# Chunk-selecting attention with a gated feed-forward layer on one core: the last block product of the program, made, added and stored in two halves of 128 columns

## The chip, the core and the metric

The program runs on one core of a Trainium2 chip. A core has five engines with a queue of instructions each: TensorE (PE in the profile; its weight loads are shown as PEld), VectorE (DVE), ScalarE (ACT), GpSimd (POOL) and SyncE (SP), which here issues nearly all transfers. Engines wait for each other through semaphores. The metric is the time of one execution on the device in microseconds (us); less is better.

## The reference, cut to what matters

```python
B, H, S, D = 4, 8, 768, 64                     # batch, heads, sequence, head dimension
# attention: each query keeps the 6 chunks of 32 keys with the highest upper bound
k_min, k_max = k_chunks.min(axis=3), k_chunks.max(axis=3)
ub = np.sum(np.maximum(q * k_min, q * k_max), axis=-1)      # causal chunks only
mask = sel & (pos[:, None] >= pos[None, :])                 # sel: the top 6 by ub
attn = softmax(where(mask, q @ k.T / 8, -1e9))
x = (attn @ v)                                 # -> 3072 tokens x 512
# feed-forward: 512 -> 1536 -> 512
gate = 1 / (1 + np.exp(-(x @ w_gate)))
out = (gate * (x @ w_val)) @ w_out             # 3072 x 512, float32
```

## The kernel before

The 3072 tokens are cut into eight units, u0 to u7, of three blocks of 128 tokens. A unit goes through chunk choice, attention and feed-forward (`ffn`, line 1239). The units' work is interleaved: a text, `ORDER`, lists every operation of the program with its engine, and the operations are issued in exactly that order. A second text, `SLOTS`, gives every tile its buffer; for most operations of TensorE this is one of the eight accumulator banks. A third text, `TIES`, adds some waits by hand. No scheduler decides anything at build time except which waits follow from these texts.

The last product of the feed-forward layer, hidden values times `w_out`, is done for units 4 to 7 on pairs of token blocks (`pair`, line 1058). Two blocks of 128 tokens times 512 columns are treated as a 2 by 2 scheme of blocks, which needs seven products instead of eight: p1, p2, p6, p5, p3, p7, p4, each with sums of hidden values (made at line 1069 into the tiles `sw` and `sx`) or of weights (`tw`). A product (line 1082) is six matmuls of 128 by 128 weights with 256 columns, which add up in one bank. VectorE then adds it onto the output tile `ox` or `sw` (function `onto`, line 1099; "c22", "c21" and so on are the names of these additions). The last pair of the program is called u67: the third blocks of units 6 and 7. The end of `ORDER` before is

```
p7_u67=P p7z_u67=P c22_u67=V out_u67_b1=S p4_u67=P p4z_u67=P c21_u67=V out_u67_1=S
```

so the last things that the program does are: product p7, the addition c22 (512 columns, as two lots of 256), the store `out_u67_b1` of the right half of the last 128 rows, product p4 (issued in two parts, `p4` and `p4z`, of four and two matmuls), the addition c21 of 256 columns, and the store `out_u67_1` of the left half of these rows. c21 reads and writes a quarter of `ox` that c22 has written, so it follows c22.

A store (line 1127) is one transfer issued on SP. Each transfer that SP issues is counted by one of eight completion counters, DMAHW0 to DMAHW7, taken in turn. Where a counter's earlier transfer has to be waited for as well, SP has a small wait instruction ahead of the transfer.

After the last store comes a closing stage that the framework adds (line 1452 in the profile, the end of the program). SP waits there for everything, two semaphores to an instruction and one instruction after another, in this order:

```
1 DMASW7, DMASW6    2 DMAHW0, DMASW5    3 DMAHW1, DMASW4
4 DMAHW2, DMASW3    5 DMAHW3, DMASW2    6 DMAHW4, DMASW1
7 DMAHW5, DMASW0    8 DMAHW6, DVE       9 DMAHW7, ACT
```

(DMASW are the counters of the transfers that GpSimd issues.) Then the five engines meet twice and the execution ends. In the program before, `out_u67_b1` is counted by DMAHW6 and the very last store, `out_u67_1`, by DMAHW7.

Of the kernel before, what the change touches and what calls it, by code (L numbers as in the profile page):

```python
# [262 lines left out]
c22_u67=V out_u67_b1=S p4_u67=P p4z_u67=P c21_u67=V out_u67_1=S  # L263
# [51 lines left out]
sc_u4_7_0:0 att_u4_7:2 sc_u4_7_1:4 pv_u4_3:1 sc_u4_7_2:4 sc_u4_7_3:2 rz_u4_3:0 x_u4_3:1 g_u4_0:3 gate_u4_0:0 v_u4_0:5 hg_u4_0:6
g_u4_1:7 gate_u4_1:2 v_u4_1:2 g_u4_2:3 gate_u4_2:1 v_u4_2:1 hg_u4_1:5 g_u4_3:3 gate_u4_3:3 v_u4_3:1 g_u4_4:6 gate_u4_4:0 v_u4_4:4
hg_u4_2:7 g_u4_5:6 gate_u4_5:2 v_u4_5:3 g_u4_6:6 gate_u4_6:2 v_u4_6:1 hg_u4_3:1 g_u4_7:7 gate_u4_7:3 v_u4_7:4 g_u4_8:7 gate_u4_8:0
v_u4_8:5 hg_u4_4:2 g_u4_9:3 gate_u4_9:1 v_u4_9:4 g_u4_10:7 gate_u4_10:1 v_u4_10:6 hg_u4_5:8 g_u4_11:6 gate_u4_11:2 v_u4_11:1
held:0 sw:1 p1_u4:7 p26_u4:1 p5_u4:7 p3_u4:2 p7_u4:4 p4_u4:6 k_3:0 q_3:1 kx_3:1 k16_3_0:4 kt_3_0:6 k16_3_1:2 kt_3_1:1 k16_3_2:3
# [77 lines left out]
def pe(busy, lag=170):  # L397
    return {PE: (busy, busy + lag)}
# [1058 lines left out]
```

## Time and profile before

| | |
|---|---|
| median of 3 runs | 281.0 us (280.67 to 282.69) |
| profiled execution: its time / its span | 279.88 us / 278.2 us |
| TensorE busy | 269.2 us, 97% of the span |
| VectorE, ScalarE, GpSimd busy | 231.2, 180.4, 163.1 us |
| granted TensorE clock | 1.0 |

The span runs from the first to the last instruction that the profiler saw; 1.7 us of the profiled execution's time lie outside it. Busy shares are averages over very different stages. For a change at the very end of the program the last few microseconds of the trace matter, and there the order of single instructions.

### The profile page before, as it was taken

Reading aid. Unit: us, or ns where it says so; the run is one execution under the profiler, and the core shown is the slowest. Engines: PE = TensorE matmul, PEld = TensorE weight load, DVE = VectorE, ACT = ScalarE, POOL = GpSimd, SP = SyncE. Lnnn points to the kernel's source line nnn. Section 1 sums busy time; section 2 is a strip of 40 time slices with the busy share of each in tenths; the row PEclk is TensorE's granted clock in tenths of the full one; section 3 lists DMA queues with packets and bytes.
Section 4 is the critical chain, followed back from the end, with each engine's and each line's share of the span. In section 5 each row is a group of like instructions: output and inputs, shape, how many; then the busy total and the mean of one; then the engine's idle time right before and its main releaser. Section 6 shows DMA issues by size and latency. Waiting matters only on the chain.

```text
span 278.2 us, 7566 instructions
## 1 busy us (share of the span) xinstructions
PE 269.2 (97%) x2806; PEld 189.3 (68%) x2806; DVE 231.2 (83%) x686; ACT 180.4 (65%) x386; POOL 163.1 (59%) x262
## 2 busy tenths in 40 slices
PE   5979999999999999999999999999999999999995
PEld 3755658667755666557687657776888688778684
DVE  4799747687999998796999987978889998888985
ACT  6388969569858944468689979988983422341430
POOL 5797744639372873534669966724766467163440
PEclk9999999999999999999999999999999999999999
DMA  6999999999999598696896230100320033000304
GB/s 157 258 281 204 207 217 208 220 179 202 187 217 189 142 183 188 145 161 125 164 157 114 68 85 17 40 0 3 73 77 2 1 83 127 2 1 2 151 2 152
DMA packets 131717, 34.70 MB, mean 125 GB/s; under 512 B 119776, under 2 KB 128736, under 8 KB 131680
## 3 DMA queue, kind: packets, MB, share of 16 engines
q1 hardware_dynamic: 126912, 29.50, 50.6%
q0 software_dynamic: 4768, 4.72, 10.1%
q8 instruction: 22, 0.36, 0.5%
q14 instruction: 15, 0.12, 0.1%
HBM read 30.67 MB, written 6.29 MB: 133 GB/s over the span
## 4 chain that ended last, share of the span: by engine, by line
PE 87%; DMA 6%; DVE 5%; SPq 1%; issue 0%; POOL 0%; DVEq 0%
PE v_u L1259 20%; PE g_u L1259 15%; PE sc_u L957 12%; PE o_u L1308 11%; PE p_u L1082 10%; PE pv_u L990 7%; DMA wg<-in_moe_w_gate_dram 5%; PE p_g_u L1191 5%; PE ube_u L896 3%; DMA kf<-in_k_dram 1%; DVE xf L768 1%; PE kfT L709 1%; PE qfT L709 1%; PE fl L591 1%; DVE kx_u L681 1%; DVE kcr L681 1%
## 5 line engine op out<-in xcount | busy, mean ns | idle before, releaser
L968 ACT ACTIVATE att_u<-sc_u 128x512 f16<-128x512 f32 (+3 forms) x184 | 86.9, 573 | 8.6 <-PE sc_u L957 7.3
L1259 PE MATMUL v_u<-xT_u,wv 128*128 128x384 f16 x384 | 72.4, 326 | 0.0
L1280 DVE SCALAR_TENSOR_TENSOR hg_u<-gate_u,v_u 128x384 f16<-128x384 f16 x96 | 51.2, 545 | 19.3 <-ACT gate_u L1271 9.7
L1271 ACT ACTIVATE gate_u<-g_u 128x384 f16<-128x384 f32 x72 | 35.1, 499 | 40.3 <-PE g_u L1259 35.1
L1259 PE MATMUL g_u<-xT_u,wg 128*128 128x384 f16 x288 | 56.0, 326 | 0.9 <-ACT xT_u L452 0.5
L1259 PEld LDWEIGHTS <-wv 128*128 128x128 f16 x384 | 36.2, 98 | 20.3 <-issue 0.2
L974 POOL TENSOR_SCALAR_AFFINE_SELECT att_u<-att_u 128x384 f16<-128x384 f16 (+1 forms) x56 | 28.0, 509 | 37.4 <-ACT att_u L968 16.4
L1259 PEld LDWEIGHTS <-wg 128*128 128x128 f16 x288 | 26.7, 98 | 18.3 <-DMA wg<-in_moe_w_gate_dram 1.8
L1308 PE MATMUL o_u<-wo,hg_u 128*128 128x512 f16 x144 | 34.3, 379 | 0.0
L990 PE MATMUL pv_u<-v,att_u 128*128 128x65 f16 x640 | 26.3, 193 | 0.0
L990 PEld LDWEIGHTS <-att_u 128*128 128x128 f16 x640 | 24.2, 98 | 2.9 <-issue 0.6
L1228 DVE TENSOR_TENSOR f_g_u<-p_g_u,f_g_u 128x192 f32<-128x192 f32 (+1 forms) x72 | 24.9, 383 | 1.0 <-PE p_g_u L1191 0.4
L957 PE MATMUL sc_u<-hqe,hke 128*128 128x128 f16 (+2 forms) x220 | 25.1, 243 | 0.0
L957 PE MATMUL sc_u<-hqo,hko 128*128 128x128 f16 (+2 forms) x220 | 24.1, 243 | 0.0
L1308 PEld LDWEIGHTS <-hg_u 128*128 128x128 f16 x144 | 13.7, 98 | 13.4
L957 PEld LDWEIGHTS <-hke 128*128 128x128 f16 x220 | 16.5, 98 | 4.9 <-issue 0.6
L957 PEld LDWEIGHTS <-hko 128*128 128x128 f16 x220 | 16.4, 98 | 4.4
L673 POOL CAST v<-v 128x512 f16<-128x512 f32 x23 | 14.4, 627 | 5.8 <-DVE qf_u L863 1.8
L1271 ACT ACTIVATE gate_u<-f_g_u 128x384 f16<-128x384 f32 x24 | 11.9, 519 | 5.6 <-DVE hg_u L1280 2.9
L1011 DVE TENSOR_TENSOR x_u<-pv_u,rz_u 128x384 f16<-128x384 f32 (+1 forms) x28 | 14.6, 524 | 0.9 <-DMA xT_u<-x_u 0.6
L919 DVE MAX8 mx_u<-ubn_u 128x8 f32<-128x8 f32 (+16 forms) x152 | 12.7, 158 | 0.3
L1099 DVE SCALAR_TENSOR_TENSOR sw<-p_u,sw 128x256 f32<-128x256 f32 (+1 forms) x20 | 10.6, 528 | 2.4 <-PE p_u L1082 2.0
(187 smaller groups left out, 504.9 us busy)
## 6 DMA issues: line engine op xcount, KB each, us to landing
v<-in_v_dram SPq DMA_DIRECT2D x23, 256.0 KB, 4.7
k<-in_k_dram SPq DMA_DIRECT2D x12, 384.0 KB, 5.4
q<-in_q_dram SPq DMA_DIRECT2D x12, 384.0 KB, 5.9
out_dram<-osb_u SPq DMA_DIRECT2D x12, 256.0 KB, 3.3
out_dram<-sw SPq DMA_DIRECT2D x8, 256.0 KB, 2.1
wv<-in_moe_w_val_dram POOLq DMA_DIRECT2D x3, 512.0 KB, 9.8
wo<-in_moe_w_out_dram POOLq DMA_DIRECT2D x3, 512.0 KB, 17.6
qf<-in_q_dram SPq DMA_DIRECT2D x8, 128.0 KB, 3.3
```

The source lines that it names most:

```text
L673: plan.add(f"v16_{b}_{ib}", {POOL: pool(H * D)}, lambda e: nc.gpsimd.tensor_copy(v16[b % 2][:, ib, :, 0:D], at(t)), reads=[t], writes=[("v ...
L957: nc.tensor.matmul(at(t)[:, o:o + 128 * m], hk[b % 2][e_][:, p, 128 * jb:128 * jb + 128], hq[u.side][e_][:, p, 128 * x:128 * (x + m)], sta ...
L968: plan.add(f"exp_{u.name}_{h}_{y}", {ACT: act(n)}, lambda e, t=t, att=att, b0=b0, n=n: nc.scalar.activation(at(att)[:, b0:b0 + n], at(t), ...
L974: nc.gpsimd.affine_select(out=dv, in_=dv, compare_op=ALU.is_ge, fill=0.0, base=0, pattern=[[0, u.m], [1, 128]], channel_multiplier=-1)
L990: nc.tensor.matmul(at(pv)[:, last, x, :], at(att)[:, c:c + 128], v16[b % 2][:, jb, h, :], start=(jb == 0), stop=(jb == ib))
L1011: plan.add(f"x_{u.name}_{p}", {DVE: dve(u.t)}, lambda e: nc.vector.tensor_tensor(at(x_).rearrange("p a (e d) -> p e a d", e=2), at(pv)[:, ...
L1082: nc.tensor.matmul(at(to)[:, side], a(j)[:, i], b(j)[:, i], start=j == i == 0, stop=j == 2 and i == 1)
L1228: plan.add(f"{p}_{name}", {POOL: pool2(192 * n), DVE: dve(192 * n)} if slow else {DVE: dve(192 * n)}, lambda e: both(e).tensor_tensor(dst( ...
L1259: nc.tensor.matmul(at(t), w16[:, c, 128 * fb:128 * fb + 128], at(u.xt)[:, c, :], start=(c == 0), stop=(c == 3))
L1271: plan.add(f"tanh_{u.name}_{fb}", {ACT: act(T, not seven[0])}, lambda e, gv=gv, gate=gate: nc.scalar.activation(at(gate), gv(), AF.Tanh, s ...
L1280: plan.add(f"hg_{u.name}_{fb}", {DVE: dve(T)}, lambda e, vv=vv, gate=gate, hg=hg, fb=fb: nc.vector.scalar_tensor_tensor(at(hg)[:, fb % 2], ...
L1308: nc.tensor.matmul(at(o), at(hgs[fc // 2])[:, fc % 2, 128 * tb:128 * tb + 128], wo16[:, fc, lo:hi], start=(fc == 0), stop=(fc == NFB - 1))
```

## The change

The product p4 of pair u67 is made as two products of 128 columns, `p4` and `p4b`, each of six matmuls, in two accumulator banks. Each has its own addition (c21, c21b) of 128 columns and its own store (`out_u67_1`, `out_u67_1b`) of 128 rows by 128 columns, 64 KB. `out_u67_b1` stays as it was. Stores, products and additions of all other pairs stay as they were.

```diff
-c22_u67=V out_u67_b1=S p4_u67=P p4z_u67=P c21_u67=V out_u67_1=S
+c22_u67=V out_u67_b1=S p4_u67=P p4b_u67=P c21_u67=V c21b_u67=V out_u67_1=S out_u67_1b=S
...
         if name == "u67":
             store(f"{name}_b1", lambda: four()[:, 3], rows[1], 256, 512, [key[3]], next_)
-            store(f"{name}_1", lambda: four()[:, 2], rows[1], 0, 256, [key[2]], next_)
+            for side, cut, last in (("", slice(0, 128), p4), ("b", slice(128, 256), bank("p4b"))):
+                def emit(e, cut=cut, last=last):
+                    for j in range(3):
+                        for i in range(2):
+                            nc.tensor.matmul(at(last)[:, 0, cut], block(j, 1, 1)[:, i], t_(3)(j)[:, i, cut],
+                                             start=j == i == 0, stop=j == 2 and i == 1)
+                plan.add(f"p4{side}_{name}", pe(...), emit, reads=[...], writes=[last], prio=next_())
+                done = key[2] if side == "" else (okey, 2, side)
+                plan.add(f"c21{side}_{name}", {DVE: dve(128)}, lambda e, cut=cut, last=last: nc.vector.scalar_tensor_tensor(
+                    four()[:, 2, cut], at(last)[:, 0, cut], 0.5, four()[:, 2, cut], ALU.mult, ALU.add),
+                    reads=[last, key[2]], writes=[done], prio=next_(EV))
+                store(f"{name}_1{side}", lambda cut=cut: four()[:, 2, cut], rows[1], cut.start, cut.stop, [done], next_)
```

Up to the last product, no engine's order of operations changes. What does change in the whole program is `SLOTS`: 496 of its 1053 old entries have another number, nearly all of them accumulator banks. A bank decides which earlier tile has to be read out before a product may write. Setting the two built programs side by side, 65 of the 655 matmuls that wait for something wait for another event than before; on ScalarE one wait falls away, and on VectorE, GpSimd and SP nothing differs ahead of c21. Since the counters are taken in turn, the store `out_u67_1` is counted by DMAHW7 and the new last store, `out_u67_1b`, by DMAHW0.

More of the change, by code (lines that the diff above doesn't have):

```diff
@@ L316 @@
[L316 to L319, printed above, removed]
@@ new lines @@
+kT_u1_1:3 kt_u1_1:0 kn_u1_2:0 kT_u1_2:1 kt_u1_2:0 kn_u1_3:1 kT_u1_3:1 kt_u1_3:2 qn_u1_0:5 qT_u1_0:0 qf_u1:0 qm_u1:0 qn_u1_1:0
+qT_u1_1:5 qn_u1_2:4 qT_u1_2:6 qn_u1_3:6 qT_u1_3:0 ube_u1:5 ubo_u1:7 ubn_u1:0 mx_u1:0 apt_u1:0 g_u0_0:2 gate_u0_0:0 v_u0_0:3
+hg_u0_0:0 g_u0_1:6 gate_u0_1:3 v_u0_1:1 g_u0_2:4 gate_u0_2:1 v_u0_2:5 hg_u0_1:1 g_u0_3:0 gate_u0_3:2 v_u0_3:4 g_u0_4:6 gate_u0_4:0
+v_u0_4:0 hg_u0_2:3 g_u0_5:7 gate_u0_5:3 v_u0_5:2 g_u0_6:1 gate_u0_6:2 v_u0_6:3 hg_u0_3:2 g_u0_7:5 gate_u0_7:1 v_u0_7:4 g_u0_8:4
@@ new lines @@
+gate_u0_8:0 v_u0_8:7 hg_u0_4:5 g_u0_9:5 gate_u0_9:2 v_u0_9:6 g_u0_10:3 gate_u0_10:1 v_u0_10:0 hg_u0_5:4 g_u0_11:6 gate_u0_11:3
+v_u0_11:3 o_u0_0:4 osb_u0_0:0 o_u0_1:5 osb_u0_1:1 o_u0_2:0 osb_u0_2:0 kq_u2:1 v_0_4:5 v_0_5:4 kf_3:3 qf_3:1 vf_3:0 kn_u2_0:4
+kT_u2_0:5 kx_u2:0 kt_u2_0:0 kn_u2_1:0 kT_u2_1:7 kt_u2_1:1 kn_u2_2:6 kT_u2_2:6 kt_u2_2:1 kn_u2_3:0 kT_u2_3:1 kt_u2_3:2 qn_u2_0:3
+qT_u2_0:3 qf_u2:1 qm_u2:0 qn_u2_1:1 qT_u2_1:6 qn_u2_2:6 qT_u2_2:4 qn_u2_3:5 qT_u2_3:1 ube_u2:3 ubo_u2:7 ubn_u2:0 mx_u2:0 apt_u2:0
@@ new lines @@
+sc_u1_0_0:1 att_u1_0:1 sc_u1_0_1:2 sc_u1_0_2:6 sc_u1_1_0:7 att_u1_1:3 sc_u1_1_1:6 pv_u1_0:0 sc_u1_1_2:0 sc_u1_2_0:5 att_u1_2:2
+sc_u1_2_1:5 rz_u1_0:1 x_u1_0:0 xps_u1_0:1 xT_u1:1 sc_u1_2_2:0 sc_u1_3_0:1 att_u1_3:0 sc_u1_3_1:2 pv_u1_1:7 sc_u1_3_2:3 sc_u1_4_0:3
+att_u1_4:2 sc_u1_4_1:4 rz_u1_1:0 x_u1_1:2 xps_u1_1:4 sc_u1_4_2:5 sc_u1_5_0:4 att_u1_5:0 sc_u1_5_1:1 pv_u1_2:0 sc_u1_5_2:2
+sc_u1_6_0:4 att_u1_6:3 sc_u1_6_1:2 rz_u1_2:0 x_u1_2:1 xps_u1_2:2 sc_u1_6_2:7 sc_u1_7_0:3 att_u1_7:1 sc_u1_7_1:2 pv_u1_3:0
@@ new lines @@
+sc_u1_7_2:5 rz_u1_3:1 x_u1_3:2 xps_u1_3:0 g_u1_0:5 gate_u1_0:0 v_u1_0:7 hg_u1_0:6 g_u1_1:2 gate_u1_1:1 v_u1_1:5 g_u1_2:0
+gate_u1_2:2 v_u1_2:4 hg_u1_1:7 g_u1_3:0 gate_u1_3:3 v_u1_3:0 g_u1_4:1 gate_u1_4:0 v_u1_4:2 hg_u1_2:8 g_u1_5:0 gate_u1_5:0 v_u1_5:1
+g_u1_6:5 gate_u1_6:2 v_u1_6:3 hg_u1_3:0 g_u1_7:0 gate_u1_7:2 v_u1_7:5 g_u1_8:3 gate_u1_8:1 v_u1_8:4 hg_u1_4:2 g_u1_9:4 gate_u1_9:3
+v_u1_9:2 g_u1_10:6 gate_u1_10:0 v_u1_10:7 hg_u1_5:1 g_u1_11:0 gate_u1_11:3 v_u1_11:6 o_u1_0:3 osb_u1_0:0 o_u1_1:1 osb_u1_1:1
@@ new lines @@
+xps_u2_1:2 sc_u2_4_2:3 sc_u2_5_0:6 att_u2_5:3 sc_u2_5_1:2 pv_u2_2:7 sc_u2_5_2:5 sc_u2_6_0:3 att_u2_6:3 sc_u2_6_1:6 rz_u2_2:1
+x_u2_2:0 xps_u2_2:7 sc_u2_6_2:1 sc_u2_7_0:2 att_u2_7:1 sc_u2_7_1:3 pv_u2_3:4 sc_u2_7_2:5 rz_u2_3:1 x_u2_3:0 xps_u2_3:7 kfT_3:0
+kf16_3:4 qfT_3:2 qf16_3:1 vh_3:2 scf_3_0:4 scf_3_1:1 attf_3_0:0 pvf_3_0:4 rzf_3_0:0 xf_3_0:0 xpsf_3_0:4 attf_3_1:2 pvf_3_1:7
+rzf_3_1:1 xf_3_1:1 xpsf_3_1:7 g_u2_0:2 gate_u2_0:0 v_u2_0:5 hg_u2_0:3 g_u2_1:7 gate_u2_1:2 v_u2_1:7 g_u2_2:1 gate_u2_2:1 v_u2_2:4
@@ new lines @@
+ubo_u4:3 ubn_u4:0 mx_u4:0 apt_u4:0 v_2_0:4 v_2_1:3 sc_u3_0_0:4 att_u3_0:1 sc_u3_0_1:0 sc_u3_0_2:0 sc_u3_1_0:2 att_u3_1:2
+sc_u3_1_1:5 pv_u3_0:0 sc_u3_1_2:3 sc_u3_2_0:3 att_u3_2:3 sc_u3_2_1:7 rz_u3_0:1 x_u3_0:1 xT_u3:1 sc_u3_2_2:6 sc_u3_3_0:4 att_u3_3:3
+sc_u3_3_1:7 pv_u3_1:1 sc_u3_3_2:3 sc_u3_4_0:2 att_u3_4:0 sc_u3_4_1:4 rz_u3_1:0 x_u3_1:2 sc_u3_4_2:0 sc_u3_5_0:7 att_u3_5:2
+sc_u3_5_1:6 pv_u3_2:2 sc_u3_5_2:5 sc_u3_6_0:6 att_u3_6:0 sc_u3_6_1:4 rz_u3_2:0 x_u3_2:2 sc_u3_6_2:3 sc_u3_7_0:4 att_u3_7:1
@@ new lines @@
+sc_u3_7_1:7 pv_u3_3:3 sc_u3_7_2:5 rz_u3_3:1 x_u3_3:0 g_u3_0:5 gate_u3_0:3 v_u3_0:2 hg_u3_0:8 g_u3_1:1 gate_u3_1:2 v_u3_1:3
+g_u3_2:0 gate_u3_2:0 v_u3_2:2 hg_u3_1:1 g_u3_3:1 gate_u3_3:3 v_u3_3:4 g_u3_4:0 gate_u3_4:2 v_u3_4:3 hg_u3_2:2 g_u3_5:2 gate_u3_5:1
+v_u3_5:7 g_u3_6:0 gate_u3_6:1 v_u3_6:7 hg_u3_3:3 g_u3_7:2 gate_u3_7:3 v_u3_7:2 g_u3_8:7 gate_u3_8:2 v_u3_8:4 hg_u3_4:4 g_u3_9:6
+gate_u3_9:1 v_u3_9:3 g_u3_10:7 gate_u3_10:0 v_u3_10:2 hg_u3_5:0 g_u3_11:4 gate_u3_11:3 v_u3_11:0 o_u3_0:2 osb_u3_0:0 o_u3_1:4
@@ new lines @@
+osb_u3_1:1 o_u3_2:3 osb_u3_2:1 qf_u5:1 qf_u6:0 qm_u5:0 ube_u5:6 ubo_u5:4 ubn_u5:0 mx_u5:0 apt_u5:0 v_2_2:3 v_2_3:5 v_2_4:4 tw:0
+sc_u4_0_0:3 att_u4_0:1 sc_u4_0_1:0 sc_u4_0_2:7 sc_u4_0_3:6 sc_u4_1_0:7 att_u4_1:1 sc_u4_1_1:0 pv_u4_0:5 sc_u4_1_2:2 sc_u4_1_3:3
+sc_u4_2_0:1 att_u4_2:0 sc_u4_2_1:0 rz_u4_0:1 x_u4_0:1 xT_u4:0 sc_u4_2_2:7 sc_u4_2_3:7 sc_u4_3_0:0 att_u4_3:0 sc_u4_3_1:7 pv_u4_1:1
+sc_u4_3_2:3 sc_u4_3_3:6 sc_u4_4_0:5 att_u4_4:3 sc_u4_4_1:0 rz_u4_1:0 x_u4_1:2 sc_u4_4_2:6 sc_u4_4_3:3 sc_u4_5_0:3 att_u4_5:2
@@ new lines @@
+sc_u4_5_1:2 pv_u4_2:3 sc_u4_5_2:7 sc_u4_5_3:7 sc_u4_6_0:5 att_u4_6:0 sc_u4_6_1:2 rz_u4_2:1 x_u4_2:0 sc_u4_6_2:0 sc_u4_6_3:3
+sc_u4_7_0:1 att_u4_7:2 sc_u4_7_1:2 pv_u4_3:6 sc_u4_7_2:2 sc_u4_7_3:6 rz_u4_3:0 x_u4_3:1 g_u4_0:4 gate_u4_0:0 v_u4_0:1 hg_u4_0:6
+g_u4_1:0 gate_u4_1:2 v_u4_1:5 g_u4_2:7 gate_u4_2:1 v_u4_2:6 hg_u4_1:5 g_u4_3:4 gate_u4_3:3 v_u4_3:6 g_u4_4:2 gate_u4_4:0 v_u4_4:4
+hg_u4_2:7 g_u4_5:2 gate_u4_5:2 v_u4_5:4 g_u4_6:2 gate_u4_6:2 v_u4_6:6 hg_u4_3:1 g_u4_7:0 gate_u4_7:3 v_u4_7:4 g_u4_8:0 gate_u4_8:0
@@ new lines @@
+v_u4_8:1 hg_u4_4:2 g_u4_9:7 gate_u4_9:1 v_u4_9:4 g_u4_10:0 gate_u4_10:1 v_u4_10:2 hg_u4_5:8 g_u4_11:2 gate_u4_11:2 v_u4_11:6
+held:0 sw:1 p1_u4:0 p26_u4:6 p5_u4:6 p3_u4:5 p7_u4:3 p4_u4:1 k_3:0 q_3:1 kx_3:1 k16_3_0:4 kt_3_0:2 k16_3_1:6 kt_3_1:1 k16_3_2:3
+kt_3_2:0 k16_3_3:5 kt_3_3:3 qm_u6:0 ube_u6:6 ubo_u6:0 ubn_u6:0 mx_u6:0 apt_u6:0 v_2_5:0 v_3_0:0 v_3_1:1 v_3_2:2 sc_u5_0_0:4
+att_u5_0:1 sc_u5_0_1:0 sc_u5_0_2:2 sc_u5_1_0:5 att_u5_1:3 sc_u5_1_1:1 pv_u5_0:4 sc_u5_1_2:0 sc_u5_2_0:3 att_u5_2:2 sc_u5_2_1:3
@@ new lines @@
+rz_u5_0:1 x_u5_0:0 xT_u5:1 sc_u5_2_2:5 sc_u5_3_0:1 att_u5_3:0 sc_u5_3_1:7 pv_u5_1:7 sc_u5_3_2:0 sc_u5_4_0:0 att_u5_4:3 sc_u5_4_1:6
+rz_u5_1:0 x_u5_1:2 sc_u5_4_2:5 sc_u5_5_0:7 att_u5_5:1 sc_u5_5_1:3 pv_u5_2:1 sc_u5_5_2:1 sc_u5_6_0:0 att_u5_6:0 sc_u5_6_1:5
+rz_u5_2:1 x_u5_2:1 sc_u5_6_2:6 sc_u5_7_0:2 att_u5_7:2 sc_u5_7_1:0 pv_u5_3:5 sc_u5_7_2:7 rz_u5_3:0 x_u5_3:0 qf_u7:1 qm_u7:0
+ube_u7:3 ubo_u7:7 ubn_u7:0 mx_u7:0 apt_u7:0 v_3_3:5 v_3_4:3 v_3_5:2 sc_u6_0_0:2 att_u6_0:1 sc_u6_0_1:0 sc_u6_0_2:1 sc_u6_1_0:6
@@ new lines @@
+att_u6_1:3 sc_u6_1_1:7 pv_u6_0:7 sc_u6_1_2:1 sc_u6_2_0:6 att_u6_2:2 sc_u6_2_1:0 rz_u6_0:0 x_u6_0:1 xT_u6:0 sc_u6_2_2:7 sc_u6_3_0:5
+att_u6_3:3 sc_u6_3_1:6 pv_u6_1:4 sc_u6_3_2:4 sc_u6_4_0:4 att_u6_4:1 sc_u6_4_1:1 rz_u6_1:0 x_u6_1:0 sc_u6_4_2:0 sc_u6_5_0:6
+att_u6_5:3 sc_u6_5_1:2 pv_u6_2:4 sc_u6_5_2:4 sc_u6_6_0:6 att_u6_6:0 sc_u6_6_1:2 rz_u6_2:1 x_u6_2:2 sc_u6_6_2:3 sc_u6_7_0:4
+att_u6_7:3 sc_u6_7_1:7 pv_u6_3:3 sc_u6_7_2:4 rz_u6_3:1 x_u6_3:2 ss_g1:0 ss_g2:4 ss_g3:1 ss_g4:3 g_u5_0:1 gate_u5_0:2 v_u5_0:6
@@ new lines @@
+hg_u5_0:3 g_u5_1:3 gate_u5_1:0 v_u5_1:3 p1_g1_u5:0 f0_g1_u5:5 f1_g1_u5:1 p26_g1_u5:6 p53_g1_u5:3 p74_g1_u5:1 gate_u5_2:3 v_u5_2:3
+hg_u5_1:0 gate_u5_3:0 v_u5_3:0 p1_g2_u5:3 f0_g2_u5:6 f1_g2_u5:4 p26_g2_u5:6 p53_g2_u5:0 p74_g2_u5:5 gate_u5_4:1 v_u5_4:1 hg_u5_2:4
+gate_u5_5:1 v_u5_5:3 p1_g3_u5:6 f0_g3_u5:2 f1_g3_u5:5 p26_g3_u5:3 p53_g3_u5:7 p74_g3_u5:0 gate_u5_6:0 v_u5_6:4 hg_u5_3:1
+gate_u5_7:2 v_u5_7:1 p1_g4_u5:0 f0_g4_u5:0 f1_g4_u5:3 p26_g4_u5:4 p53_g4_u5:4 p74_g4_u5:1 gate_u5_8:1 v_u5_8:1 hg_u5_4:7
@@ new lines @@
+gate_u5_9:3 v_u5_9:0 g_u5_10:0 gate_u5_10:3 v_u5_10:5 hg_u5_5:5 g_u5_11:4 gate_u5_11:0 v_u5_11:4 p1_u5:1 p26_u5:4 p5_u5:3 p3_u5:4
+p7_u5:7 p4_u5:2 sx:1 p1_u45:5 ox:0 p26_u45:4 p5_u45:2 p3_u45:4 p7_u45:2 p4_u45:1 g_u6_0:1 gate_u6_0:0 v_u6_0:4 hg_u6_0:2 g_u6_1:2
+gate_u6_1:0 v_u6_1:4 p1_g1_u6:7 f0_g1_u6:0 f1_g1_u6:5 p26_g1_u6:5 p53_g1_u6:1 p74_g1_u6:0 gate_u6_2:2 v_u6_2:1 hg_u6_1:6
+gate_u6_3:1 v_u6_3:1 p1_g2_u6:3 f0_g2_u6:3 f1_g2_u6:5 p26_g2_u6:5 p53_g2_u6:0 p74_g2_u6:7 gate_u6_4:3 v_u6_4:1 hg_u6_2:8
@@ new lines @@
+gate_u6_5:2 v_u6_5:4 p1_g3_u6:3 f0_g3_u6:6 f1_g3_u6:2 p26_g3_u6:3 p53_g3_u6:7 p74_g3_u6:6 gate_u6_6:1 v_u6_6:3 hg_u6_3:4
+gate_u6_7:0 v_u6_7:6 p1_g4_u6:1 f0_g4_u6:4 f1_g4_u6:1 p26_g4_u6:4 p53_g4_u6:5 p74_g4_u6:3 gate_u6_8:2 v_u6_8:4 hg_u6_4:3
+gate_u6_9:1 v_u6_9:4 g_u6_10:2 gate_u6_10:3 v_u6_10:4 hg_u6_5:7 g_u6_11:3 gate_u6_11:0 v_u6_11:1 p1_u6:4 p26_u6:1 p5_u6:6 p3_u6:5
+p7_u6:2 p4_u6:3 sc_u7_0_0:4 att_u7_0:0 sc_u7_0_1:5 sc_u7_0_2:6 sc_u7_0_3:1 sc_u7_1_0:7 att_u7_1:3 sc_u7_1_1:4 pv_u7_0:2
+sc_u7_1_2:2 sc_u7_1_3:2 sc_u7_2_0:2 att_u7_2:1 sc_u7_2_1:6 rz_u7_0:1 x_u7_0:1 xT_u7:1 sc_u7_2_2:2 sc_u7_2_3:1 sc_u7_3_0:4
@@ new lines @@
+att_u7_3:3 sc_u7_3_1:6 pv_u7_1:7 sc_u7_3_2:4 sc_u7_3_3:5 sc_u7_4_0:0 att_u7_4:2 sc_u7_4_1:6 rz_u7_1:1 x_u7_1:0 sc_u7_4_2:0
+sc_u7_4_3:1 sc_u7_5_0:3 att_u7_5:1 sc_u7_5_1:5 pv_u7_2:6 sc_u7_5_2:0 sc_u7_5_3:4 sc_u7_6_0:2 att_u7_6:0 sc_u7_6_1:5 rz_u7_2:0
+x_u7_2:2 sc_u7_6_2:4 sc_u7_6_3:0 sc_u7_7_0:1 att_u7_7:0 sc_u7_7_1:0 pv_u7_3:1 sc_u7_7_2:6 sc_u7_7_3:7 rz_u7_3:0 x_u7_3:1 g_u7_0:6
+gate_u7_0:3 v_u7_0:7 hg_u7_0:0 g_u7_1:7 gate_u7_1:1 v_u7_1:0 p1_g1_u7:5 f0_g1_u7:3 f1_g1_u7:1 p26_g1_u7:2 p53_g1_u7:5 p74_g1_u7:7
@@ new lines @@
+gate_u7_2:1 v_u7_2:2 hg_u7_1:1 gate_u7_3:2 v_u7_3:5 p1_g2_u7:2 f0_g2_u7:0 f1_g2_u7:2 p26_g2_u7:1 p53_g2_u7:5 p74_g2_u7:7
+gate_u7_4:0 v_u7_4:0 hg_u7_2:5 gate_u7_5:2 v_u7_5:7 p1_g3_u7:7 f0_g3_u7:4 f1_g3_u7:5 p26_g3_u7:6 p53_g3_u7:3 p74_g3_u7:2
+gate_u7_6:1 v_u7_6:3 hg_u7_3:8 gate_u7_7:3 v_u7_7:6 p1_g4_u7:1 f0_g4_u7:6 f1_g4_u7:1 p26_g4_u7:6 p53_g4_u7:0 p74_g4_u7:4
+gate_u7_8:3 v_u7_8:3 hg_u7_4:2 gate_u7_9:2 v_u7_9:6 g_u7_10:5 gate_u7_10:0 v_u7_10:2 hg_u7_5:3 g_u7_11:0 gate_u7_11:1 v_u7_11:4
+p1_u7:2 p26_u7:5 p5_u7:0 p3_u7:1 p7_u7:4 p4_u7:7 p1_u67:1 p26_u67:6 p5_u67:3 p3_u67:2 p7_u67:5 p4_u67:0 p4b_u67:1
@@ L1117, in pair @@
         onto("c22", p7, 2, slice(2, 4), lambda: four()[:, 2:4], [key[2], key[3]])
-        product("p4", p4, 0, lambda j: block(j, 1, 1), t_(3), lambda j: h(1, 1)(j) + [(tw, 3, j)])
-        onto("c21", p4, 1, slice(2, 3), lambda: four()[:, 2:3], [key[2]])
         if name == "u67":
             store(f"{name}_b1", lambda: four()[:, 3], rows[1], 256, 512, [key[3]], next_)
-            store(f"{name}_1", lambda: four()[:, 2], rows[1], 0, 256, [key[2]], next_)
-        else:
+            for side, cut, last in (("", slice(0, 128), p4), ("b", slice(128, 256), bank("p4b"))):
+                def emit(e, cut=cut, last=last):
+                    for j in range(3):
+                        for i in range(2):
+                            nc.tensor.matmul(at(last)[:, 0, cut], block(j, 1, 1)[:, i], t_(3)(j)[:, i, cut], start=j == i == 0, stop=j == 2 and i == 1)
+                plan.add(f"p4{side}_{name}", pe(6 * (128 / 2.4 + 4.5)), emit, reads=[r for j in range(3) for r in h(1, 1)(j) + [(tw, 3, j), ("wo", j)]],
+                         writes=[last], prio=next_())
+                done = key[2] if side == "" else (okey, 2, side)
[3 more added lines that the diff above has]
+                store(f"{name}_1{side}", lambda cut=cut: four()[:, 2, cut], rows[1], cut.start, cut.stop, [done], next_)
+        else:
+            product("p4", p4, 0, lambda j: block(j, 1, 1), t_(3), lambda j: h(1, 1)(j) + [(tw, 3, j)])
+            onto("c21", p4, 1, slice(2, 3), lambda: four()[:, 2:3], [key[2]])
             store(f"{name}_1", lambda: four()[:, 2:4], rows[1], 0, 512, [key[2], key[3]], next_)
```

94 lines of the change are left out of this document (14 added, 80 removed).

## The prediction

> **What bounds the kernel now.** I read the first page for the shares, then the chain that ended last, then the last 6 us instruction by instruction, because the change touches nothing that runs earlier, apart from the banks.
>
> ```profile
> span 278.2 us, 7566 instructions
> PE 269.2 (97%) x2806; PEld 189.3 (68%) x2806; DVE 231.2 (83%) x686; ACT 180.4 (65%) x386; POOL 163.1 (59%) x262
> PE 87%; DMA 6%; DVE 5%; SPq 1%; issue 0%; POOL 0%; DVEq 0%
> ```
>
> TensorE is the bound for the body: 97% busy, 87% of the chain. But the end is not TensorE's. The chain's last stretch, in order of time (start, length, what):
>
> ```profile
> 272.95 1.32 PE p_u L1082 x12
> 274.27 0.02 issue
> 274.30 0.70 DVE ox L1099
> 275.00 0.03 issue
> 275.02 0.02 DVEq L1099
> 275.04 0.04 issue
> 275.09 0.42 DVE ox L1099
> ```
>
> The 12 matmuls are p3's and p7's; the 0.70 is c22, the 0.42 is c21. Product p4 does not appear: VectorE goes from c22 straight to c21 (0.09 us for its own wait). The next rows are p4's six matmuls and the three last stores on SP, then the stores' times from issue to landing (a window on the store of 256 KB, then one on the very last store), and last the closing waits on SP.
>
> ```profile
> 274.10 0.82 PE L1082 MATMUL p_u<-tw,hg_u 128*128 128x256 f16 x6
> 274.11 0.33 SPq L1127 DMA_DIRECT2D out_dram<-ox  x1
> 275.01 0.33 SPq L1127 DMA_DIRECT2D out_dram<-ox  x1
> 275.54 0.33 SPq L1127 DMA_DIRECT2D out_dram<-ox  x1
> ...
> DMA to landing us min/median/max: 2.0/2.0/2.0
> ...
> DMA to landing us min/median/max: 1.7/1.7/1.7
> ...
> L1452 SPq EVENT_SEMAPHORE  x7: 28/28/28, 275.9 to 276.3; - x7
> ...
> L1452 SPq EVENT_SEMAPHORE  x1: 28/28/28, 277.3 to 277.3; - x1
> ...
> SPq L1452 <- DMA out_dram<-ox: 0.9, 2, 0.5
> ```
>
> p4 ends at 274.10 + 0.82 = 274.92, before c22 at 275.00. The last store is issued at 275.54, as soon as c21 is done (275.09 + 0.42 = 275.51), and lands 1.7 us later, at 277.26. The closing waits start at 275.9. Seven of them pass between 275.9 and 276.3, so one takes (276.3 - 275.9)/6, about 0.07 us, when nothing holds it. Two are held by stores (0.9 us in all): the eighth by `out_u67_b1`, the ninth, at 277.3, by the very last store. The span ends 278.2 - 277.3 = 0.9 us after that. So the end is set by: c22, c21, issue, landing, and what comes after the wait that sees the landing.
>
> **The change, part by part.** *Products.* Twelve matmuls of 128 columns replace six of 256. Bodies of that size stand in the trace:
>
> ```profile
> 42.52 0.39 PE L957 MATMUL sc_u<-hqo,hko 128*128 128x128 f16 x4
> L957 PE MATMUL sc_u<-hqo,hko 128*128 128x128 f16 x148 | 16.1, 219 | 0.0
> ```
>
> Four in 0.39 us, one being 0.219 long: each starts (0.39 - 0.219)/3 = 0.057 us after the one before, each with its own weights. So p4 would run from 274.10 to 274.10 + 5 x 0.057 + 0.22 = 274.60, and p4b to 274.10 + 11 x 0.057 + 0.22 = 274.95. Both are done before c22 ends at 275.00. The product's cost is 0, hidden under c22; if that cover were gone, the price would be 274.95 - 274.92 = 0.03 us.
>
> *Additions.* VectorE rows of the two sizes, and four short independent operations in a row:
>
> ```profile
> L1099 DVE SCALAR_TENSOR_TENSOR ox<-p_u,ox 128x512 f32<-128x512 f32 x2 | 1.4, 691 | 0.4 <-PE p_u L1082 0.4
> L1099 DVE SCALAR_TENSOR_TENSOR ox<-p_u,ox 128x256 f32<-128x256 f32 x3 | 1.3, 425 | 0.3
> ...
> 267.67 0.28 DVE L1069 TENSOR_TENSOR sx<-held,hg_u 128x256 f16<-128x256 f16 x1
> 267.87 0.28 DVE L1069 TENSOR_TENSOR sw<-hg_u,sw 128x256 f16<-128x256 f16 x1
> ```
>
> 256 columns more cost 0.691 - 0.425 = 0.266, so 128 columns take 0.425 - 0.133 = 0.292 us. c21 still waits for c22 and starts at 275.09; it ends at 275.38 instead of 275.51. c21b works on other columns and has no wait on c21; independent operations start 0.08 before the one before them ends (0.20 apart at 0.28 each), so it runs from 275.30 to 275.59. If it does not overlap, 275.67.
>
> *Issues on SP.* This is where the gain of c21 goes. `out_u67_b1` holds SP from 275.01 to 275.34. Ahead of the next store stands a wait for its counter. How close two issues can follow:
>
> ```profile
> L1127 SPq EVENT_SEMAPHORE  x21: 17/17/17, 52.0 to 275.4; - x21
> L1127 SPq DMA_DIRECT2D out_dram<-sw x2: 333/379/425, 272.2 to 272.6; - x2
> ...
> 272.20 0.81 SPq L1127 DMA_DIRECT2D out_dram<-sw  x2
> ```
>
> The two stores at 272.2 have no wait instruction between them: 0.81 - 0.425 - 0.333 = 0.05 us of gap. With a wait instruction there are two such gaps, and one of 0.017 us: 0.09 taken, bounds 0.05 and 0.12. So `out_u67_1` can go at 275.34 + 0.09 = 275.43 (c21 is done by then), 0.11 earlier than the last store now. It holds SP to 275.76 (0.33 was the same for 128 and 256 KB, and the rows are 128 again). `out_u67_1b` goes at 275.85; c21b, done at 275.59 or 275.67, does not bind. The last issue moves from 275.54 to 275.85: +0.31 us (bounds 0.27 and 0.37).
>
> *Landing.* 256 KB took 2.0 us and 128 KB 1.7, so 0.3 per 128 KB; 64 KB less is 0.15 less: 1.55. No store of 64 KB stands in the trace. Bounds: 1.7 (no shorter than 128 KB) and 1.4 (as large a step again). I take 1.55, the same slope. The last landing comes at 275.85 + 1.55 = 277.40 instead of 277.26: +0.14 us, bounds -0.05 and +0.36.
>
> The Trainium skill, "DMA: Bandwidth & Descriptors", section "Anatomy of one DMA", speaks against cutting stores up: a transfer costs about 2.0 us whatever its size, and beyond that only its bytes at 436 GB/s. By that fit 64 KB would land after 2.15 us (an estimate from the page), at 278.00, and the sum below would be +1.3 instead of +0.7. Its slope, 0.15 us for 64 KB, agrees with the rows; its fixed part does not, since 128 KB landed in 1.7 where it gives 2.3 (the page fits GpSimd's path). The rows decide.
>
> *Closing waits.* The last landing now counts on DMAHW0, which the second of the nine closing waits asks for, not on DMAHW7, which the ninth asks for. SP therefore stands at the second wait until 277.40 and has seven more to go through after it, 0.07 us each: +0.49 us on the path. Today these seven pass at 275.9 to 276.3 under the landing; the change takes this cover away. Bounds: 0 (waits whose events are long past cost nothing then) and 7 x 0.09 = 0.63.
>
> *The banks.* I set the 65 changed waits of TensorE against the times at which the trace shows their new events. Two of these waits fall away, and 61 of the new events come at least 0.1 us before the matmul starts in the trace. Two come after:
>
> ```profile
> 20.87 0.47 ACT L452 CAST kt_u<-kT_u 128x384 f16<-128x384 f32 x1
> 21.14 0.28 PE L775 MATMUL xpsf<-ident,xf 128*128 128x128 f16 x2
> 22.82 1.76 PE L1259 MATMUL g_u<-xT_u,wg 128*128 128x384 f16 x8 [0.51 <-ACT xT_u L452]
> ...
> 209.70 0.36 DVE L1228 TENSOR_TENSOR f_g_u<-p_g_u,f_g_u 128x192 f32<-128x192 f32 x1
> 210.02 0.33 PE L1191 MATMUL p_g_u<-hko,ss_g 128*128 128x192 f16 x2
> ```
>
> At 21.14 a transpose would wait for ScalarE until 21.34, 0.2 us; TensorE sits idle for 0.51 us ahead of 22.82, which hides it. At 210.02 a product would wait for VectorE until 210.06: +0.05 us in a dense stretch, taken as lost (bounds 0 and 0.1).
>
> *Sum.* 0.14 (landing) + 0.49 (closing waits) + 0.05 (bank) = +0.68, say +0.7 us. The span goes to 278.9 and the profiled execution from 279.88 to 280.6. The runs shown lie higher, with a median of 281.0; on their scale I predict 281.7 us. The profiled execution is 1.1 us below that median and the runs spread over 2.0, so the loss should be visible in the trace and barely in the times. One per cent, 2.8 us, is about what a measurement of this kernel can tell from no change.
>
> **The rivals.** *The closing waits cost nothing* (chance 0.15). SP reads semaphores whose events are past as fast as it can, and the step of 0.07 might be there only because the queue was being filled. Against it: seven such steps with nothing to wait for took 0.4 us. Then +0.14 + 0.05: 281.2 us.
>
> *A small store lands no sooner than one of 128 KB* (0.18). For it: half the bytes saved only 0.3 of 2.0 us. The last landing is then 275.85 + 1.7 = 277.55, +0.29, and with closing and bank +0.83: 281.8 us. By the skill's fit it would be the 2.15 above.
>
> *The tail gets shorter* (0.06): not slower than before. The place is the landing: if a store's time after its issue is mostly its rows' bytes on their way, 64 KB lands in 1.4 us. This decides only if the closing steps are free too. 275.85 + 1.4 = 277.25, so -0.01, and with the tighter issue gaps of 0.05 twice, 275.34 + 0.05 + 0.33 + 0.05 = 275.77, -0.09: 280.9 us. Against it: SP cannot issue the second store less than 0.33 after the first.
>
> *The dealt-out banks stall TensorE* (0.06): slower by over 1%. The 61 harmless new waits have 0.1 us or more to spare in one execution. If VectorE or ScalarE runs later than there by more than that, products wait in a queue that has no idle time to hide it. A loss of 2.8 us needs about 0.04 us at each of the 63. Then 0.7 + 2.8: 284.5 us. Against it: VectorE, GpSimd and SP have the same waits as before, so their lateness should not change.
>
> **How the numbers follow.** The forecast has 0.55, the rivals 0.15, 0.18, 0.06 and 0.06. The forecast and the first three rivals all lie within 1% of 281.0. The bounds of the sum alone are -0.1 (the shorter tail) and 0.36 + 0.63 + 0.1 = +1.1, so 280.9 to 282.1 from 281.0. The level of a median of a few runs is unsure by more: the runs shown go 0.3 below it and 1.7 above. From 280.9 - 0.6 to 282.1 + 1.0 gives 280.3 to 283.1. Faster by over 1% has 0.02, slower 0.06 (the last rival), within 1% 0.92.
>
> **What would show each step.** In the changed profile: twelve matmuls ending by 274.95 on the old time scale; c21 and c21b of about 0.29 us with c21b starting before c21 ends; three issues on SP about 0.42 apart with the last 0.31 later than now; a landing of about 1.55 us for the last one; and one closing wait at the start, a long hold, then eight starts of closing waits 0.07 apart after the landing, with the span's end 1.4 us behind it instead of 0.9. I am wrong if the span shrinks, if the hold still stands at the ninth wait, or if TensorE shows new idle time of more than 0.3 us in the body.

## The result, and the profile after

The changed kernel takes 282.16 us (median of 17 runs, 281.55 to 283.71) against 281.03 for the kernel before (17 runs): a ratio of 1.0041 with a 95% interval of 1.0025 to 1.0057, that is 0.7 to 1.6 us more, around 1.15. One run of the kernel before, at 287.94 us, was in a slower state and is left out of the ratio. The change makes the kernel slower by less than 1%.

The profiled execution has a span of 280.5 us against 278.2. That difference of 2.3 us must not be read as the change's: about half of it lies in the first 60 us, where executions of any of these kernels differ (more on that below). So the end is compared from one event, the end of product p7, at which c22 starts. From there to the span's end it is 3.91 us before and 5.00 us after. The chain's last stretch of the changed kernel, in order of time:

```profile
269.93 5.58 PE p_u L1082 x51
275.51 0.02 issue
275.54 0.70 DVE ox L1099
276.24 0.03 issue
276.27 0.02 DVEq L1129
276.29 0.04 issue
276.33 0.29 DVE ox L1129
276.63 0.20 DVEq L1464
```

c22 runs from 275.54 to 276.23, c21 starts 0.10 us after it as before and takes 0.29. The two half products on TensorE, and VectorE's last three rows:

```profile
275.34 0.50 PE L1124 MATMUL p_u<-tw,hg_u 128*128 128x128 f16 x6
275.67 0.50 PE L1124 MATMUL p4b_u<-tw,hg_u 128*128 128x128 f16 x6
```

```profile
275.54 0.69 DVE L1099 SCALAR_TENSOR_TENSOR ox<-p_u,ox 128x512 f32<-128x512 f32 x1 [0.21 <-PE p_u L1082]
276.33 0.29 DVE L1129 SCALAR_TENSOR_TENSOR ox<-p_u,ox 128x128 f32<-128x128 f32 x1
276.54 0.28 DVE L1129 SCALAR_TENSOR_TENSOR ox<-p4b_u,ox 128x128 f32<-128x128 f32 x1
```

Both halves are made by 276.17, under c22; c21b starts before c21 ends and is done at 276.82. The last three stores on SP, each from a window of its own:

```profile
276.26 0.33 SPq L1139 DMA_DIRECT2D out_dram<-ox  x1
...
276.68 0.38 SPq L1139 DMA_DIRECT2D out_dram<-ox  x1
...
277.15 0.40 SPq L1139 DMA_DIRECT2D out_dram<-ox  x1
```

The very last store goes out 0.33 us after its columns are ready, because SP is still busy with the others. Its time to landing, and the closing waits in three windows: before its landing, just after, and the rest:

```profile
DMA to landing us min/median/max: 1.6/1.6/1.6
...
L1464 SPq EVENT_SEMAPHORE  x1: 28/28/28, 277.6 to 277.6; - x1
...
L1464 SPq EVENT_SEMAPHORE  x4: 28/28/28, 278.8 to 279.0; - x4
...
L1464 SPq EVENT_SEMAPHORE  x4: 28/28/28, 279.4 to 279.6; - x4
```

The store lands at 278.78. One wait stands ahead of it, at 277.6; the second is held until 278.8; and seven more follow, up to 279.6. Between the fourth of the second lot, at 279.0, and the next, at 279.4, there is a gap of 0.40 us. From the landing to the last closing wait it is 0.83 us, where it was 0.02 before.

### The profile page after: what moved, and what is told of

The parts are those of the page before. It is cut to its first block, busy times and chain, and to the rows that moved or that the text cites. A ratio compares the mean times of both kernels' runs of the same rounds, so it can differ in the third digit from the quotient of the medians.

```text
span 280.5 us, 7583 instructions
## 1 busy us (share of the span) xinstructions
PE 270.8 (97%) x2812; PEld 191.3 (68%) x2812; DVE 231.6 (83%) x687; ACT 180.7 (64%) x386; POOL 163.2 (58%) x262
## 4 chain that ended last, share of the span: by engine, by line
PE 86%; DMA 8%; DVE 2%; SPq 2%; issue 0%; POOL 0%; DVEq 0%; POOLq 0%
PE v_u L1271 20%; PE g_u L1271 15%; PE sc_u L957 12%; PE o_u L1320 11%; PE p_u L1082 10%; PE pv_u L990 7%; PE p_g_u L1203 5%; DMA wg<-in_moe_w_gate_dram 5%; PE ube_u L896 3%; DMA kq_u<-in_k_dram 2%; DMA kf<-in_k_dram 1%; SPq L647 1%; PE kfT L709 1%; PE kT_u L795 1%; PE qT_u L795 1%; PE qfT L709 0%
```

## The experiments

All times "from p7" below are taken from one trace each, from the end of product p7 to the span's end. c22 ends 0.71 us after p7 in every trace but the last two, so an expectation that counts from c22's end is 0.71 less. Ratios are against runs of the kernel before from the same round; the experiments have 12 runs each.

| kernel | from p7, us | ratio (95% interval) |
|---|---|---|
| before | 3.91 | |
| changed | 5.00 | 1.0041 (1.0025 to 1.0057) |
| e1: before, last store on DMAHW0 | 4.79 | 1.0023 (0.9996 to 1.0049) |
| e2: changed, last store on DMAHW7 | 4.73 | 1.0041 (1.0014 to 1.0067) |
| e3: changed, one store | 3.94 | 0.9999 (0.9972 to 1.0026) |
| e4: changed, banks of before | 5.00 | 1.0032 (1.0005 to 1.0058) |
| e5: changed, DMAHW7, SP's step moved off | 4.17 | 1.0032 (1.0000 to 1.0063) |
| e6: changed, last store on ScalarE's queue | 4.80 | 1.0033 (1.0013 to 1.0054) |
| e7: before, c22 split | 4.32 | 1.0036 (1.0014 to 1.0059) |
| e8: e7, SP's step moved | 3.85 | 1.0004 (0.9978 to 1.0031) |

The times alone separate only the larger differences. The traces show the smaller ones too, but each is one execution. The changed kernel and e4, whose ends are the same, agree at 5.00; how much a second trace of the others would differ is not shown.

**e1: nothing but the counter.** One earlier store of the kernel before is cut in two, so that every later transfer counts one counter further on.

```diff
+        cuts = 2 if name == "u3_0" else 1
+        rows_ = 128 // cuts
-        plan.add(f"out_{name}", {SP: (350, 350)}, lambda e: nc.sync.dma_start(
-            out[r:r + 128, lo:hi], src()), ...)
+        plan.add(f"out_{name}", {SP: (350, 350)}, lambda e: [nc.sync.dma_start(
+            out[r + rows_ * i:r + rows_ * (i + 1), lo:hi], src()[rows_ * i:rows_ * (i + 1)]) for i in range(cuts)], ...)
```

> The kernel before, with one earlier store (out_u3_0, at about 231 us, where SP is idle) issued as two pieces of 64 rows. Nothing else changes, but the last two stores now count on DMAHW7 and DMAHW0 instead of DMAHW6 and DMAHW7. Theory (the closing waits stand on the path): from the end of c22 to the span's end 3.2 us becomes 3.2 + 0.8 = 4.0 us (the changed kernel showed 0.8 us from the last landing to the last closing wait), 281.8 us against 281.0. Rival (closing waits are free, the loss is the late store): 3.2 us, 281.0.

Measured: 4.79 us from p7 against 3.91, +0.88. VectorE, the stores and their landings stand as before; the closing waits do not:

```profile
L1454 SPq EVENT_SEMAPHORE  x9: 28/28/28, 276.6 to 278.8; - x9
...
L1454 SPq EVENT_SEMAPHORE  x5: 28/28/28, 277.9 to 278.2; - x5
...
L1454 SPq EVENT_SEMAPHORE  x3: 28/28/28, 278.6 to 278.8; - x3
...
SPq L1454 <- DMA out_dram<-ox: 1.3, 1, 1.3
```

One wait at 276.6, then a single hold of 1.3 us, then eight in two lots with a gap of 0.4 between 278.2 and 278.6. The place at which the closing stage asks for the last store's counter is worth 0.88 us with nothing else changed at the end. In the trace, half of that (0.44) is six steps of the usual size from one wait to the next, and the other half (0.43) is the one long step. The rival with free closing waits falls.

**e2: the counter put back.** The same edit on the changed kernel with `cuts = 8`: seven transfers more, so the last store is back on DMAHW7.

> The changed kernel, with out_u3_0 issued as eight pieces of 16 rows, so that the last store counts on DMAHW7 again. Theory: the closing waits pass under the landing as before, so the part from c22's end to the span's end, 4.27 us in the changed kernel, becomes 4.27 - 0.8 = 3.5 us; 281.3 us. Rival (the late store alone makes the loss): stays at 4.3 us and 282.2.

Measured: 4.73, where 4.2 (3.5 from c22's end) was expected and 5.0 by the rival. Neither is right. The closing waits do pass under the landing, but the last store is late:

```profile
276.36 0.81 SPq L1141 DMA_DIRECT2D out_dram<-ox  x2
...
277.63 0.33 SPq L1141 DMA_DIRECT2D out_dram<-ox  x1
...
DMA to landing us min/median/max: 1.8/1.8/1.8
...
L1466 SPq EVENT_SEMAPHORE  x8: 27/28/28, 278.0 to 278.5; - x8
...
L1466 SPq EVENT_SEMAPHORE  x1: 28/28/28, 279.5 to 279.5; - x1
```

It goes out at 277.63, which is 0.46 us after SP was free (276.36 + 0.81 = 277.17); in the changed kernel the same distance is 0.09. This makes 0.37 us of the excess over the expectation. The landing adds 0.19: this store of 64 KB took 1.82 us, and the changed kernel's 1.62; no run shows why. The eight waits show no gap. The step of 0.4 us has moved from the closing waits to the front of the last store. Counting SP's instructions in the traces, it lies in the same place in the before, the changed, e1, e2, e3 and e4 kernels: between the 207th and the 208th that the trace shows, whatever these are (0.39 to 0.43 us between two waits, and in e2 the 0.37 us more at the store). In the kernel before, the 208th is the eighth closing wait, which I had put down to the landing of `out_u67_b1`. In that trace the step and the landing end together and cannot be told apart. e3 has the same order at its end, and there the eighth wait passes 0.08 us after that landing, where a wait that a landing holds passes 0.02 after it: the step is what ends last.

**e3: halves made and added, one store.**

```diff
-                store(f"{name}_1{side}", lambda cut=cut: four()[:, 2, cut], rows[1], cut.start, cut.stop, [done], next_)
+            store(f"{name}_1", lambda: four()[:, 2], rows[1], 0, 256, [key[2], (okey, 2, "b")], next_)
```

> The changed kernel with both halves made and added as they are, but stored by one transfer of 128 x 256, counted by DMAHW7. Theory: the two additions end 0.07 us later than one of 256 columns and nothing else is lost, so 3.18 + 0.07 = 3.25 us from c22's end to the span's end, 281.1 us. Rival (making the product in halves costs, through TensorE or the banks): 281.5 or more.

Measured: 3.94 against 3.91, and a ratio of 0.9999. The two additions end 0.07 us later than the single one:

```profile
276.78 0.29 DVE L1129 SCALAR_TENSOR_TENSOR ox<-p_u,ox 128x128 f32<-128x128 f32 x1
276.99 0.28 DVE L1129 SCALAR_TENSOR_TENSOR ox<-p4b_u,ox 128x128 f32<-128x128 f32 x1
```

So making and adding in halves is nearly free; the loss is in storing in halves.

**e4: the banks of before.** The changed kernel with the old `SLOTS`, and `p4b_u67:7`.

> The changed kernel with the banks of before (p4b in bank 7). Theory (banks cost nothing measurable): body up to c22's end as before, tail as in the changed kernel, 282.1 us. Rival (the banks make part of the loss): 281.7 or less.

Measured: 5.00 from p7, as in the changed kernel. The banks have nothing to do with the tail. In the body they have a small cost. Timed by the ends of VectorE's instructions from 59 us on, the five traces with the old banks and the five with the new ones run level up to 214 us, nearly all within 0.01 us; from 216 us on those with the old banks are still level, within 0.02, and those with the new ones are 0.08 to 0.11 behind. (495 of the old entries of `SLOTS` have another number; the 496 counted above include the new `p4b_u67`.) TensorE shows where it starts: the changed kernel is 1.15 us behind the kernel before at one pair of matmuls (211.00 against 209.85) and 1.24 behind at the next, 211.26 against 210.02. This next pair is the product that the prediction named; here are the pairs in the changed kernel, the first of them in the kernel before, and both in e4:

```profile
211.00 0.33 PE L1203 MATMUL p_g_u<-hke,ss_g 128*128 128x192 f16 x2
211.26 0.32 PE L1203 MATMUL p_g_u<-hko,ss_g 128*128 128x192 f16 x2
...
209.85 0.33 PE L1191 MATMUL p_g_u<-hke,ss_g 128*128 128x192 f16 x2
...
210.73 0.33 PE L1203 MATMUL p_g_u<-hke,ss_g 128*128 128x192 f16 x2
210.90 0.33 PE L1203 MATMUL p_g_u<-hko,ss_g 128*128 128x192 f16 x2
```

The step from one pair of matmuls to the next, 0.17 us (209.85 to 210.02) before and 0.17 in e4, is 0.26 in the changed kernel: 0.09 us, which stays to the end. There the pair waits for VectorE:

```profile
210.46 0.74 DVE L1240 TENSOR_TENSOR f_g_u<-p_g_u,f_g_u 128x192 f32<-128x192 f32 x2
```

It ends at 211.20, and the matmul starts 0.06 us after that.

**e5: the counter put back, and SP's step moved away.** As e2 with `cuts = 16`: fifteen transfers more. The counter is DMAHW7 again, and the 208th instruction comes well before the last stores.

> The changed kernel with out_u3_0 issued as sixteen pieces of 8 rows: the last store counts on DMAHW7 again, and the place of SP's 0.4 us step (between its 207th and 208th recorded instruction in all six traces so far) falls well ahead of the last three stores instead of in front of the very last one. Theory (closing waits plus this step make 0.8 us of the loss): 4.29 us from c22's end to the span's end becomes 4.29 - 0.81 = 3.47. Rival (the eight-piece kernel's 4.02 was the late store itself): 4.0 again.

Measured: 4.17 from p7, that is 3.46 from c22's end where 3.47 was expected:

```profile
277.49 0.40 SPq L1141 DMA_DIRECT2D out_dram<-ox  x1
...
L1466 SPq EVENT_SEMAPHORE  x8: 28/28/28, 277.9 to 278.7; - x8
...
L1466 SPq EVENT_SEMAPHORE  x1: 28/28/28, 279.1 to 279.1; - x1
```

The last store goes out 1.64 us after p7, as in the changed kernel; eight waits pass before it lands, one after. The counter's place and SP's step together are worth 5.00 - 4.17 = 0.83 us of the changed kernel. What stays, 4.17 - 3.91 = 0.26, is the late store itself. The times (281.54 us) are too wide to say more than that they agree.

**e6: the last store on ScalarE's queue.**

```diff
-        plan.add(f"out_{name}", {SP: (350, 350)}, lambda e: nc.sync.dma_start(
+        plan.add(f"out_{name}", {SP: (350, 350)}, lambda e: (nc.scalar if name == "u67_1b" else nc.sync).dma_start(
```

> The changed kernel with only the very last store issued on ScalarE's queue; it still counts on DMAHW0. Theory: it is issued as soon as c21b is done, 0.62 us after c22's end instead of 0.93, lands 0.3 us earlier, and the closing waits cost their 0.83 us as before: 4.29 - 0.31 = 3.98 us from c22's end to the span's end. Rival (the serial issue on SP does not matter): 4.29.

Measured: 4.80 from p7, 4.08 from c22's end, against 3.98 expected and 4.29 by the rival.

```profile
276.18 0.81 SPq L1139 DMA_DIRECT2D out_dram<-ox  x2
276.25 0.29 DVE L1129 SCALAR_TENSOR_TENSOR ox<-p_u,ox 128x128 f32<-128x128 f32 x1
276.46 0.28 DVE L1129 SCALAR_TENSOR_TENSOR ox<-p4b_u,ox 128x128 f32<-128x128 f32 x1
276.77 0.37 ACTq L1139 DMA_DIRECT2D out_dram<-ox  x1
```

The store goes out as soon as c21b is done (276.74), 0.30 us sooner, and lands 0.26 sooner. The missing 0.1: the store takes 1.67 us to land instead of 1.62, and the waits after it 0.87 instead of 0.83. That SP issues one store after another cost 0.30 us at the issue, and 0.20 of that reached the end (4.80 against 5.00). Even on a queue of its own the last half goes out later than the undivided store before, 1.34 us after p7 against 1.27, because the second addition ends later than the single one, 1.31 against 1.24.

**e7 and e8: a shorter tail.** The traces show c21 waiting for the right half of c22, which it does not need. Here c22 is two additions, the left one first, and the middle store goes on ScalarE's queue so that SP is free for the last.

```diff
-        onto("c22", p7, 2, slice(2, 4), ...)
+            for p, i in (("c22l", 2), ("c22", 3)):
+                plan.add(f"{p}_{name}", {DVE: dve(256)}, lambda e, i=i: nc.vector.scalar_tensor_tensor(
+                    four()[:, i:i + 1], at(p7), 0.5, four()[:, i:i + 1], ALU.mult, ALU.add), reads=[p7, key[i]], writes=[key[i]], ...)
...
+   (nc.scalar if name == "u67_b1" else nc.sync).dma_start(...)
```

> The kernel before with c22 as two additions of 256 columns, the left one first, and out_u67_b1 issued on ScalarE's queue; c21 and its store as before. From the end of product p7 to the span's end before: 3.91 us. Theory: c21 no longer waits for the right half of c22, ends 0.11 us earlier, and its store with it; but SP has two instructions fewer, so its 0.4 us step falls behind the last closing wait, where nothing hides it: 3.91 - 0.11 + 0.33 = 4.13 us. Rival (no such fixed place): 3.80 us.

> The same as the kernel with c22 split, with out_u3_0 issued in nine pieces, so that the counters stand as they did and SP's step falls between the first and the second closing wait, under the landing. Theory: 3.91 - 0.11 = 3.80 us from the end of p7 to the span's end, 0.1 us better than the kernel before, 281.0 us by the times. Rival (no fixed place): the same as without the pieces.

Measured: e7 4.32 (4.13 expected, 3.80 by the rival). VectorE does what was meant:

```profile
275.06 0.76 DVE L1119 SCALAR_TENSOR_TENSOR ox<-p_u,ox 128x256 f32<-128x256 f32 x2 [0.21 <-PE p_u L1082]
275.73 0.41 DVE L1099 SCALAR_TENSOR_TENSOR ox<-p_u,ox 128x256 f32<-128x256 f32 x1
```

c21 ends 1.11 us after p7 instead of 1.24. The step of SP falls behind the last closing wait, as foreseen:

```profile
L1457 SPq EVENT_SEMAPHORE  x1: 28/28/28, 278.0 to 278.0; - x1
L1457 SPq DRAIN  x1: 129/129/129, 278.4 to 278.4; - x1
```

0.4 us lie between the last wait and the drain (0.07 in the kernel before), and the drain takes 0.13 instead of 0.01. Of the 0.19 us above the expectation 0.12 is this drain and 0.07 the landing, which took 1.82 us instead of 1.73. In e8, with the nine pieces, the step lies between the first closing wait and the second, under the landing:

```profile
278.49 0.37 ACTq L1133 DMA_DIRECT2D out_dram<-ox  x1
278.82 0.33 SPq L1133 DMA_DIRECT2D out_dram<-ox  x1
...
L1458 SPq EVENT_SEMAPHORE  x1: 28/28/28, 279.2 to 279.2; - x1
...
L1458 SPq EVENT_SEMAPHORE  x6: 27/28/28, 279.6 to 279.9; - x6
```

e8 needs 3.85 us from p7 (3.80 expected): 0.06 better than the kernel before, one trace against one, and nothing in the times (1.0004). Of the 0.13 us gained at c21 about half is lost again in the landing, which takes 1.80 instead of 1.73 us. The store before it is only 0.33 ahead, where it was 0.53; that this is the reason is not shown.

## Why the prediction was right, and where its sizes were off

The direction, the rough size and the mechanism were right: a small loss, all of it in SP's last stores and closing waits and in one product. Term by term, predicted and measured (all in us):

| term | predicted | measured | where |
|---|---|---|---|
| products made in halves | 0, hidden | 0 | both done before c22 ends |
| one addition | 0.292 | 0.29, 0.28 | changed profile |
| last issue | +0.31 | +0.37 | 1.64 against 1.27 after p7 |
| landing of 64 KB | 1.55 | 1.62 | changed profile |
| issue and landing together | +0.14 | +0.27 | last landing 3.27 against 3.00 after p7 |
| closing waits | +0.49 | +0.81 | 0.83 against 0.02 after the landing |
| banks | +0.05 | +0.09 | 211.26; gone in e4 |
| sum | +0.68 | +1.17 | runs: +1.15 (0.7 to 1.6) |

*The step that was mis-sized most* is the closing waits: "it has seven more to go through after it, 0.07 us each". Three of the seven steps took 0.07, the fourth 0.40, the other three 0.06 to 0.08. I had read the step from seven free waits before; the long one stood in that same profile, between the seventh and the eighth, and I took it for the wait for a landing ("two are held by stores"). The landing was at 1.74 us after c22's end and the wait passed at 1.76, by chance just when the step ended. e2, e5, e7 and e8 show the step by moving it. The 0.81 is above this term's upper bound of 0.63, and the sum of 1.17 is above the +1.1 that all the bounds gave together. The measured time lay in the forecast's range because that range had been widened by 0.6 and 1.0 us for the level of the runs; this part is luck. The span ended 1.73 us after the landing, where the prediction's sign was 1.4.

*The late store* came out at twice its size because two terms were each off the same way. (Its upper bound, +0.36, should read +0.35: 277.61 against 277.26.) An issue takes 0.38 and 0.40 us, not 0.33, when another has just gone ahead (in the trace of before, a store of 0.425 was there to see, and I used the 0.333). And 64 KB landed in 1.62, between my 1.55 and the upper bound of 1.7; in e2 it took 1.82, above that bound. The Trainium skill's rule in "DMA: Bandwidth & Descriptors", "Anatomy of one DMA", about 2.0 us plus the bytes' time, would have given 2.15 for this landing; the run shows 1.62, so its fixed part does not hold for these stores, which SP issues; the section gives it for GpSimd's path. That cutting the store did not pay has other reasons here: the second issue, and the counter.

*The rivals.* "The closing waits cost nothing" fell with e1 (+0.88). "A small store lands no sooner than one of 128 KB" stays open: the last store landed 0.1 us sooner than the 1.73 of before in the changed kernel and in e4 (1.62, 1.63), but in e2 it took 1.82, and 128 KB took 1.69 to 1.82 in the other traces. "The tail gets shorter" did not come, and "the banks stall TensorE" came at the one place foreseen, with 0.09 us. The prediction let the matmul start the moment VectorE ends, 0.05 us late; it starts 0.06 us after that end. The other new wait with a late event, at 21 us, has left no trace that can be told from the scatter of the first 60 us.

*The level.* One and the same instruction of VectorE ends at 58.95 us in the trace of before and at 59.59 to 62.36 in the other nine, where the granted clock stands at half for 3.4 or 6.8 us between 15.7 and 24 us; the old banks have both the earliest and the latest. After that the traces agree to hundredths, but for the 0.09 us of the new banks. The profiled execution of before happened to be the quickest of the ten, so the sum on its scale (280.6) was too low and the one on the runs' scale was the right one to use.

## What to carry to other kernels

The end of a program is a chain of its own: last store, landing, and a fixed list of waits on the issuing queue. One more transfer anywhere ahead turns the counters, and here that alone moved the end by 0.88 us: the waits that had passed under the landing, and SP's long step among them, came to stand behind it. Before cutting or adding a transfer, look at which wait of the list the last one will answer to. Splitting a last piece so that its first half can leave earlier paid nothing here: the last half decides the end, its addition ends later than the undivided one, and on SP it queues behind the first.

## What the runs showed of the hardware that I had not expected

SP's queue stood still for about 0.4 us between two instructions, at the same count of its instructions in nine of ten traces (in the tenth, e5, a long wait covers the place): between two waits (0.39 to 0.43 us), ahead of a store (0.37 more) or ahead of the closing drain. That its place is fixed by the count is shown by e2, e7 and e8, where it moved with the number of instructions ahead; in e5 it is gone from the end.

The same traces show it a second time: in all ten, 0.42 to 0.44 us lie between SP's 79th instruction and its 80th, where 0.03 to 0.07 are usual from one instruction to the next when nothing has to be waited for. 79 and 207 are 128 apart. And in all ten a transfer of 8 KB on the queue that the profile lists as `q14 instruction` starts 1.01 to 1.09 us after the 207th instruction ends (at 277.38 us in the kernel before, at 280.05 in the changed kernel, at 262.6 in e5). So the step seems to belong to blocks of 128 instructions. Why SP stands still there is open: the transfer comes after the step and not during it, and no run here tells more.
